# Attention by head pairs: q and k loaded with features along partitions, scores in 64-row halves

## The chip, the cores and the metric

The kernel runs on one core of a Trainium2 chip. Its time is the device time of one launch in microseconds (us); the number given for a kernel is the median of its runs, here three. A profile is one execution recorded by the hardware. Its engines are PE (TensorE matmul; PEld is its weight loads), DVE (VectorE), ACT (ScalarE), POOL (GpSimd) and SP (SyncE, which issues the DMAs).

## The reference

Causal attention over B, H, S, D = 4, 8, 576, 64 is mixed with a read from a memory matrix; two feed-forward layers follow. All inputs are fp32 except the last layer's weights, which come as 64-bit words.

```python
scores = where(causal, -1e9, q @ k.T / sqrt(D)); a = softmax(scores); local = a @ v
q_p = phi(q)                                  # phi(x) = where(x > 0, x, exp(x) - 1) + 1
mem_out = (q_p @ M_prev) / (q_p . z_prev + 1e-6)
attn = g * mem_out + (1 - g) * local          # g = sigmoid(beta), one per head
x = attn as (2304, 512)                       # tokens x features
P = exp(x @ w_gate - max); 8 rounds of scaling P by its row sums and column sums
out = sum_e P[:, e] * (relu(x @ w1[e]) @ w2[e])
return leaky_relu(out @ w_in) @ w_out
```

## The kernel before, in words

Every fp32 operand of a matmul is split into a rounded part "h" and the rest "l"; a product takes three matmuls, h·h, h·l and l·h. ACT makes the rounded part by a copy to fp32r, and DVE or POOL subtracts to get the rest.

Class Attention works on 16 pairs of heads (4 batches of 4 pairs), one head (j = 0, 1) at a time. `load` fetches q, k, v token by token, in runs of 64 numbers. `transposed` turns q, k and the features phi(q) on PE and splits them. `scores` computes five blocks of rows t = 0..4 of a head: t = 0 to 3 are 128 rows each against all keys up to them, t = 4 is the tail: the last 128 rows (448 to 575), whose first half repeats rows of t = 3. In batch 0 a score block takes three matmuls; later batches stack the two parts of k on the two halves of the partitions (`stacked`), and two matmuls do. `softmax` adds the mask and takes the row maximum in one DVE instruction per block and then the exponential on ACT. `normalize` scales the blocks by the reciprocal sums, `turn` transposes the weights of the head before in three groups ("r", "x", "y") on PE, with ACT and DVE making the two parts, `outputs` multiplies them with v and adds the memory read, and `collect` puts the result into xh, xl and DRAM.

`body` runs it in stages. In the first, attention of batch 0 has the core alone, with weight pieces of expert 0 being split beside it (`W.advance`). From ("done", 0) on, `fill` puts steps of class First (expert 0's first layer, m1_products at L514, and second layer, m2_products at L522, 256 tokens at a time) between the attention steps, as many as `FILL` says per step and as far as the finished batches reach (`ready`). After attention come the gate and the Sinkhorn rounds, again with what is left of First as filler, and then `rest`, which has experts 1 to 7 and the last layer.

PSUM in the first stage: three "big" tiles of two banks and two "one" tiles of one bank. In the second: two big, one "one", two for po and one for ph (L1073, L1074, L1090). Outside `rest` the Tile framework orders each engine's instructions itself by its own estimates and priorities, so the order of the code isn't the order on an engine.

Of the kernel before, what the change touches and what calls it, by code (L numbers as in the profile page):

```python
# [27 lines left out]
def f32(ap):  # L28
    return ap.bitcast(F32)
# [31 lines left out]
class Attention:  # L61
# [4 lines left out]
    def __init__(self, tc, ctx, xh, xl, xd, q, k, v, M_prev, z_prev, ident, g_bc, iomg_bc):  # L66
        self.tc, self.nc = tc, tc.nc
        self.xh, self.xl, self.xd = xh, xl, xd
        self.q, self.k, self.v, self.M, self.z = q, k, v, M_prev, z_prev
        self.ident, self.g, self.iomg = ident, g_bc, iomg_bc  # L70
# [7 lines left out]
        self.at = {}  # L78
        for nm, pad, n in (("r", 128, 384), ("x", 64, 512), ("y", 128, 768)):
            hi = self.sb.tile([P, pad + n], F32R, name=f"at_{nm}h")  # L80
            lo = self.sb.tile([P, pad + n], F32R, name=f"at_{nm}l")
            for t in (hi, lo):
                nc.vector.memset(f32(t[:, :pad]), 0.0)
            self.at[nm] = (hi, lo, pad, n)


        self.nv = self.sb.tile([P, 5, 2, D], F32, name="nv")
        nc.gpsimd.memset(self.nv[:D, 4], 0.0)


        self.ks = [self.sb.tile([P, S], F32R, name=f"k{j}") for j in range(2)]
        self.qz = [[self.sb.tile([P, S], F32R, name=f"q{part}{j}") for part in "hl"] for j in range(2)]
        self.ms = [self.sb.tile([P, P], F32R, name=f"ms{j}") for j in range(2)]
        for j in range(2):
            for t in (*self.qz[j], self.ms[j]):
                nc.gpsimd.memset(f32(t[D - j * D:P - j * D]), 0.0)
# [4 lines left out]
    ones = "rx"  # L101

    def one(self, nm):
        return self.ps1.tile([P, 512], F32, tag="one", name=nm)

# [3 lines left out]
    def load(self, b, hp):  # L109
        nc, h0 = self.nc, 2 * hp  # L110
        r = {"b": b, "hp": hp}
        for nm, src in (("q", self.q), ("k", self.k), ("v", self.v)):
            t = self.nv if nm == "v" else self.sbt([P, 5, 2, D], "n" + nm)
            for j in range(2):
                nc.sync.dma_start(out=t[:, 0:4, j, :], in_=src[b, h0 + j, 0:512, :].rearrange("(c p) d -> p c d", p=P))
            o = D if nm == "v" else 0
            nc.sync.dma_start(out=t[o:, 4], in_=src[b, h0:h0 + 2, S - P + o:S, :].rearrange("h p d -> p h d"))
            r[nm] = t
            if nm == "q":
                z = self.sbt([P, 2, D], "nz")  # L120
                nc.sync.dma_start(out=z, in_=self.z[b:b + 1, h0:h0 + 2].to_broadcast([P, 2, D]))
        m = self.sbt([P, D], "nm")
        nc.sync.dma_start(out=m, in_=self.M[b, h0:h0 + 2].rearrange("h p d -> (h p) d"))
        r["z"], r["m"] = z, m
        return r

    def transposed(self, r, nm):

        nc = self.nc
        ps = self.big("tps")  # L130
        for c in range(5):
            q0 = 448 if c == 4 else c * P
            nc.tensor.transpose(ps[:, P + q0:2 * P + q0], r[nm[0]][:, c].rearrange("p h d -> p (h d)"), self.ident)
        rows = (slice(0, D), slice(D, P))
        stacked = self.stacked(r)
        if nm == "qT":
            for j, ((hi, lo), s) in enumerate(zip(self.qz, rows)):
                nc.scalar.activation(hi[s], ps[s, P:P + S], AF.Copy)
                if stacked:
                    nc.sync.dma_start(out=f32(hi[rows[1 - j]]), in_=f32(hi[s]))  # L140
            for (hi, lo), s in zip(self.qz, rows):
                nc.vector.tensor_sub(lo[s], ps[s, P:P + S], f32(hi[s]))
        elif nm == "kT" and stacked:
            for t, s in zip(self.ks, rows):
                nc.scalar.activation(t[s], ps[s, P:P + S], AF.Copy)
            for j, (t, s) in enumerate(zip(self.ks, rows)):
                nc.vector.tensor_sub(t[rows[1 - j]], ps[s, P:P + S], f32(t[s]))
        else:
            hi, lo = self.ks if nm == "kT" else [self.sbt([P, S], "pT" + part, F32R) for part in "hl"]
            nc.scalar.activation(hi, ps[:, P:P + S], AF.Copy)  # L150
            nc.vector.tensor_sub(lo, ps[:, P:P + S], f32(hi))
            r[nm] = hi, lo

    @staticmethod
    def stacked(r):
        return r["b"] > 0

    def features(self, r):

        nc = self.nc  # L160
        ph, z, h0 = r["q"], r["z"], 2 * r["hp"]
        r["p"] = ph
# [14 lines left out]
        nc.gpsimd.tensor_mul(ph3, ph3, nrm.rearrange("p c h -> p (c h)").unsqueeze(2).to_broadcast([P, 10, D]))  # L177

    def values(self, r):

        nc = self.nc
        vs = self.sbt([P, 2, 5, P], "vs", F32R)
        for j in range(2):
            o = D if j else 0
            nc.vector.tensor_copy(vs[:, j, :, o:o + D], r["v"][:, :, j, :])
            nc.gpsimd.tensor_sub(vs[:, j, :, D - o:P - o], r["v"][:, :, j, :], f32(vs[:, j, :, o:o + D]))
        for j, ms in enumerate(self.ms):
            o, s = (D if j else 0), slice(j * D, (j + 1) * D)
            nc.vector.tensor_copy(ms[s, o:o + D], r["m"][s])
            nc.vector.tensor_sub(ms[s, D - o:P - o], r["m"][s], f32(ms[s, o:o + D]))  # L190
        r["vs"] = vs

    def head(self, r, j):
        sm, nm = self.sbt([P, 5], "sm", bufs=2), self.sbt([P, 5], "nm_", bufs=2)
        return {"r": r, "j": j, "a": {}, "sm": sm, "nm": nm}

    def scores(self, s, t, ps, o):

        nc, r, j = self.nc, s["r"], s["j"]
        q0 = 448 if t == 4 else t * P  # L200
        n = S if t == 4 else (t + 1) * P
        (qh, ql), (ka, kb) = self.qz[j], self.ks
# [5 lines left out]
    def softmax(self, s, t, ps, o):  # L208
        nc = self.nc
        n = S if t == 4 else (t + 1) * P  # L210
        a = self.sbt([P, n], f"a{t}", bufs=2)
        mo = 64 if t == 4 else 512 - P * t
        nm, sm = s["nm"][:, t:t + 1], s["sm"][:, t:t + 1]
        nc.vector.tensor_tensor_reduce(out=a, in0=ps[:, o:o + n], in1=self.mask[:, mo:mo + n], scale=-0.125, scalar=3.0e38,  # L214
                                       op0=ALU.add, op1=ALU.min, accum_out=nm)
        nc.scalar.activation(a, a, AF.Exp, bias=nm, scale=-1.0, accum_out=sm)  # L216
        s["a"][t] = a

    def normalize(self, s, t0, t1):
        nc, h = self.nc, 2 * s["r"]["hp"] + s["j"]  # L220
        sl = s["sm"][:, t0:t1]
        nc.vector.tensor_scalar(out=sl, in0=sl, scalar1=1e-9, scalar2=self.iomg[:, h:h + 1], op0=ALU.add, op1=ALU.mult)
        nc.vector.reciprocal(sl, sl)
        for t in range(t0, t1):
            a = s["a"][t]
            if t < 3:
                nc.vector.tensor_scalar(out=a, in0=a, scalar1=s["sm"][:, t:t + 1], scalar2=None, op0=ALU.mult)
            else:
                nc.scalar.activation(a, a, AF.Copy, scale=s["sm"][:, t:t + 1])  # L229

    BLOCKS = {"r": ((1, 1), (0, 0), (1, 0)),
              "x": ((3, 3), (4, 3), (2, 0), (3, 0), (4, 0)),
              "y": ((4, 4), (2, 1), (3, 1), (4, 1), (2, 2), (3, 2), (4, 2))}

    def turn(self, s, nm):

        nc = self.nc
        hi, lo, pad, n = self.at[nm]
        ps = self.one("atps") if nm in self.ones else self.big("atps")
        o = b = 64 if nm == "y" else 0  # L240
# [937 lines left out]
```

## Time and profile before

| | us |
|---|---|
| median of 3 runs | 2236.69 (2234.03 to 2238.33) |
| profiled execution, from its first to its last instruction | 2234.6 |
| PE busy / DVE busy / ACT busy / POOL busy | 2165.0 / 1562.9 / 870.0 / 1108.8 |
| first matmul of First; first matmul of the gate; first matmul of `rest` | 113.4; 417.5; 522.2 |

No time of the profiled execution outside its span is given; the span lies 2.1 us under the median and inside the range of the runs, and it is what the sums are made against. A matmul's record holds a pipeline time beside its columns and overlaps the next record, so PE's work is read from the distance of starts and not from the busy time. Durations on other engines overlap a little too.

### The profile page before, as it was taken

The page shows a single profiled execution, that of the slowest core. Times are in us where ns is not written, and L with a number is a line of the kernel's source. Part 1 is how long each engine was busy: PE and PEld are TensorE (multiplying, and loading weights), DVE is VectorE, ACT ScalarE, POOL GpSimd, SP SyncE. Part 2 cuts the span into 40 slices and gives each one's busy share as a digit, 9 for nine tenths or more (in the row PEclk, how much of TensorE's full clock was granted, in tenths as well). Part 3 has the DMA queues.
Part 4 walks back from the last instruction along what each step waited for, and adds up shares of the span by engine and source line. Part 5 has one row for each costly group of instructions (what it writes and reads, how often), then busy time and mean ns, then how long its engine had stood idle before and what let it go on. Part 6 is the DMA issues. An engine that isn't in the chain of part 4 may idle for free.

```text
span 2234.6 us, 36326 instructions
## 1 busy us (share of the span) xinstructions
PE 2165.0 (97%) x13973; PEld 1938.1 (87%) x13973; DVE 1562.9 (70%) x2904; ACT 870.0 (39%) x1753; POOL 1108.8 (50%) x993
## 2 busy tenths in 40 slices
PE   6799999989999999999999999999999999999999
PEld 5688889778888999998998988889898988898898
DVE  8989899565877777777777788855555554566565
ACT  7877777433332222223222233332333233332421
POOL 5132222244775455455444568854555543665550
PEclk9999999999999999999999999999999999999999
DMA  5233332224542222222124634421111152336111
GB/s 138 63 89 94 92 96 82 68 90 147 161 142 67 67 67 76 76 67 67 57 71 152 213 116 135 125 72 52 57 51 45 57 201 68 109 95 227 66 57 38
DMA packets 215757, 213.01 MB, mean 95 GB/s; under 512 B 71968, under 2 KB 169248, under 8 KB 214048
## 3 DMA queue, kind: packets, MB, share of 16 engines
q1 hardware_dynamic: 215584, 210.69, 30.4%
q8 instruction: 110, 1.80, 0.3%
q14 instruction: 63, 0.52, 0.1%
HBM read 157.83 MB, written 49.28 MB: 93 GB/s over the span
## 4 chain that ended last, share of the span: by engine, by line
PE 76%; DVE 9%; issue 5%; ACT 4%; POOL 4%; DMA 2%; SPq 0%; POOLq 0%; DVEq 0%; ACTq 0%
PE po L882 35%; PE pq L839 27%; PE pq L827 4%; PE ph L514 3%; PE po L522 2%; PE sps L206 2%; PE atps L245 1%; ACT a L229 1%; PE avps L261 1%; POOL stl L687 1%; DVE a L214 1%; ACT a L216 1%; DMA xa<-xd 1%; DVE x L277 1%; ACT x L270 0%
## 5 line engine op out<-in xcount | busy, mean ns | idle before, releaser
L882 PE MATMUL po<-w,hh 128*128 128x512 f32 x2592 | 810.6, 393 | 7.9 <-ACT acc L894 3.1
L882 PEld LDWEIGHTS po<-w,hh 128*128 128x128 f32 x2592 | 473.9, 188 | 106.2 <-DVE acc L892 3.3
L882 PE MATMUL po<-w,hl 128*128 128x512 f32 x1296 | 509.4, 393 | 0.0
L629 POOL TENSOR_TENSOR w0l<-raw,w0h 128x512 fp32r<-128x512 f32 x144 | 191.3, 1349 | 360.3 <-ACT w0h L628 360.3
L857 ACT ACTIVATE hh<-c 128x512 fp32r<-128x512 f32 x224 | 129.2, 624 | 476.0 <-DVE c L852 476.0
L882 PEld LDWEIGHTS po<-w,hl 128*128 128x128 f32 x1296 | 243.6, 188 | 56.1
L839 PE MATMUL pq<-Xh,w0h 128*128 128x256 f32 x960 | 266.2, 277 | 2.1 <-DVE uv L847 1.4
L839 PE MATMUL pq<-Xl,w0h 128*128 128x256 f32 x960 | 265.3, 276 | 0.0
L839 PE MATMUL pq<-Xh,w0l 128*128 128x256 f32 x960 | 265.1, 276 | 0.0
L858 DVE SCALAR_TENSOR_TENSOR hl<-c,hh 128x512 fp32r<-128x512 f32 x224 | 169.3, 797 | 79.3 <-ACT hh L857 79.3
L892 DVE SCALAR_TENSOR_TENSOR acc<-po,Pm,acc 128x512 f32<-128x512 f32 x252 | 178.4, 748 | 49.3 <-PE po L882 47.4
L629 POOL TENSOR_TENSOR w<-raw,w 128x512 fp32r<-128x512 f32 x144 | 199.8, 1405 | 1.7 <-ACT w L628 1.7
L847 DVE TENSOR_TENSOR uv<-pq,s 128x256 f32<-128x256 f32 x144 | 60.5, 420 | 191.8 <-ACT s L846 191.6
L839 PEld LDWEIGHTS pq<-Xh,w0h 128*128 128x128 f32 x960 | 180.1, 188 | 7.3 <-DVE uv L847 2.0
L839 PEld LDWEIGHTS pq<-Xl,w0h 128*128 128x128 f32 x960 | 180.2, 188 | 4.1
L839 PEld LDWEIGHTS pq<-Xh,w0l 128*128 128x128 f32 x960 | 180.2, 188 | 0.0
L846 ACT ACTIVATE s<-pq 128x256 f32<-128x256 f32 x144 | 54.9, 381 | 256.1 <-PE pq L839 256.0
L629 POOL TENSOR_TENSOR ql<-raw,qh 128x512 fp32r<-128x512 f32 x48 | 62.8, 1329 | 129.8 <-ACT qh L628 129.8
L861 ACT ACTIVATE hh<-c 128x512 fp32r<-128x512 f32 x64 | 40.5, 632 | 185.9 <-DVE c L860 185.9
L839 PE MATMUL pq<-Xh,w1h 128*128 128x256 f32 x384 | 106.1, 276 | 1.1 <-ACT xa L957 1.1
L839 PE MATMUL pq<-Xh,sh 128*128 128x256 f32 x384 | 106.0, 276 | 0.0
L839 PE MATMUL pq<-Xl,sh 128*128 128x256 f32 x384 | 106.0, 276 | 0.0
(325 smaller groups left out, 5557.4 us busy)
## 6 DMA issues: line engine op xcount, KB each, us to landing
raw<-in_moe_w_dram SPq DMA_DIRECT2D x136, 512.0 KB, 3.6
Xh<-kh SPq DMA_DIRECT2D x6, 1792.0 KB, 7.4
Xl<-kl SPq DMA_DIRECT2D x6, 1792.0 KB, 11.5
f<-in_moe_w_in_dram SPq DMA_DIRECT2D x16, 512.0 KB, 5.0
f<-in_moe_w_out_dram SPq DMA_DIRECT2D x16, 512.0 KB, 4.7
raw<-wide_in SPq DMA_DIRECT2D x16, 512.0 KB, 3.4
raw<-wide_out SPq DMA_DIRECT2D x16, 512.0 KB, 3.7
kh<-sth SPq DMA_DIRECT2D x12, 512.0 KB, 5.2
```

What stands on the lines that cost most here:

```text
L206: nc.tensor.matmul(ps[:, o_:o_ + kn], x[:, q0:q0 + P], y[:, k0:k0 + kn], start=(i == 0), stop=(i == len(terms) - 1))
L514: nc.tensor.matmul(ph[:, :T], wp[:, c, f0:f0 + P], x[:, c, t0:t0 + T], start=(n == 0), stop=(n == 11))
L522: nc.tensor.matmul(po, a[:, s], wp[:, c, :], start=(first and n == 0), stop=(last and n == 2))
L629: self.nc.gpsimd.tensor_sub(lo, src, f32(hi))
L827: nc.tensor.matmul(ph[:, f * SB:(f + 1) * SB], wp(a, c % 2), xp[x][:, c], start=(n == 0), stop=(n == 11))
L839: nc.tensor.matmul(b[-1][:, o:o + SB], wp(a, c), X[s][part][:, x, c], start=(n == 0), stop=(n == 5))
L846: nc.scalar.activation(s1, b[0][:, lo], AF.Copy)
L847: v.tensor_add(uv[:, 0], b[0][:, up], s1)
L857: nc.scalar.activation(hh[:, f], c, AF.Relu)
L858: v.scalar_tensor_tensor(out=hl[:, f], in0=c, scalar=0.0, in1=f32(hh[:, f]), op0=ALU.max, op1=ALU.subtract)
L882: nc.tensor.matmul(po[j], a[:, f, r], w[1, part][:, f], start=(fp == 0 and f == 0 and n == 0), stop=(fp == 1 and f == 1 and n == 2))
L892: nc.vector.scalar_tensor_tensor(out=acc[t], in0=po[j], scalar=Pm[:, t0 + t, e:e + 1], in1=acc[t], op0=ALU.mult, op1=ALU.add)
```

## The change

q and k come already laid out with the 64 features of the two heads of a pair along the 128 partitions (`lay_out`, on the host, moves numbers and computes none), so PE no longer turns them; `split` makes their parts, ACT the rounded one and POOL the rest. A pair's two heads go through the steps together. For t = 0 to 3 `scores` issues, for each of the three products, one matmul on partitions 0 to 63 for the first head and one on 64 to 127 for the second, into different banks. The tail (t = 4) holds the last 64 rows of both heads in one tile of 128 rows, with q as a block-diagonal operand (`bd`), which POOL copies together. `turn` has four groups, ordered as the score stages, each for both heads at once. The features are computed from a second, token-by-token copy of q (`qn`). The weight splits of M (L184, L185 after the change) go from DVE to POOL. q and k parts, `at` and the score tiles have one buffer each. PSUM: four big tiles in the first stage; in the second two big, two for po and two for ph, and the "one" tiles are gone.

```diff
+    def split(self, r):
+        nc = self.nc
+        for n in "qk":
+            (hi, lo), raw = self.qk[n], r["raw" + n]
+            nc.scalar.activation(hi, raw, AF.Copy)
+            nc.gpsimd.tensor_sub(lo, raw, f32(hi))
+        for t, x in zip(self.bd, self.qk["q"]):
+            for j in range(2):
+                s = slice(j * D, (j + 1) * D)
+                nc.gpsimd.tensor_copy(t[s, s], f32(x[s, 512:]))
...
-        terms = ((qh, self.ks[j]), (ql, self.ks[j])) if self.stacked(r) else ((qh, ka), (qh, kb), (ql, ka))
-        for (o_, k0, kn) in (((192, 0, 320), (512, 320, 256)) if t == 4 else ((o, 0, max(n, 256)),)):
-            for i, (x, y) in enumerate(terms):
-                nc.tensor.matmul(ps[:, o_:o_ + kn], x[:, q0:q0 + P], y[:, k0:k0 + kn], start=(i == 0), stop=(i == len(terms) - 1))
+        if ts == (4,):
+            qh, ql = self.bd
+            for o, k0, kn in ((192, 0, 320), (512, 320, 256)):
+                for i, (x, y) in enumerate(((qh, kh), (qh, kl), (ql, kh))):
+                    nc.tensor.matmul(ps[:, o:o + kn], x, y[:, k0:k0 + kn], start=(i == 0), stop=(i == 2))
+            return
+        for n, t in enumerate(ts):
+            w = max((t + 1) * P, 256)
+            for i, (x, y) in enumerate(((qh, kh), (qh, kl), (ql, kh))):
+                for j in range(2):
+                    s, o = slice(j * D, (j + 1) * D), 512 * j + 256 * n
+                    nc.tensor.matmul(ps[:, o:o + w], x[s, t * P:(t + 1) * P], y[s, :w], start=(i == 0), stop=(i == 2))
...
-        group(512, 256, 320, ((0, "x", 256, 320), (3, "x", 0, 256), (1, "y", 256, 320), (2, "y", 576, 320), (4, "y", 0, 256)))
+        group(512, 256, 320, ((0, 64, 320), (1, 384, 320), (2, 704, 320), (3, 1088, 256), (4, 0, 64)))
...
+    STAGES = ((0, 1), (2,), (3,), (4,))
...
+            for k, ts in enumerate(self.STAGES):
+                lo = self.turn(prev, ts) if prev is not None else None
+                yield 1
+                self.scores(r, ts)
+                self.softmax(r, ts)
+                if lo:
+                    lo()
+                if k:
+                    next(f, None)
+                yield 2 if k < 3 else 4
+            if nxt is not None:
+                self.split(nxt)
+                if n + 2 < len(pairs):
+                    self.load_qk(pairs[n + 2])
+            if prev is not None:
+                self.outputs(prev, 0)
+            self.normalize(r)
+            if prev is not None:
+                self.collect(prev, 0)
+            yield 5
...
-FILL = {1: 1, 2: 2, 3: 2, 4: 1, 5: 1, 6: 1, 7: 2}
+FILL = {1: 1, 2: 2, 4: 2, 5: 2, 7: 2}
...
-                with tc.tile_pool(name="pa0", bufs=3, space=PSUM) as att.ps, tc.tile_pool(name="pb0", bufs=2, space=PSUM) as att.ps1:
+                with tc.tile_pool(name="pa0", bufs=4, space=PSUM) as att.ps:
...
-                fph = fx.enter_context(tc.tile_pool(name="e_ph", bufs=1, space=PSUM))
+                fph = fx.enter_context(tc.tile_pool(name="e_ph", bufs=2, space=PSUM))
...
-                with tc.tile_pool(name="pa1", bufs=2, space=PSUM) as att.ps, tc.tile_pool(name="pb1", bufs=1, space=PSUM) as att.ps1:
+                with tc.tile_pool(name="pa1", bufs=2, space=PSUM) as att.ps:
```

On PE, one head of the second stage stood like this (sps are scores, atps the turned weights of the head before, ph and po the first and second layer of First):

```order
L514 MATMUL ph<-xh,w0l_207 128x256
L245 MATMUL atps<-ident,a_1503 128x128
...
L206 MATMUL sps<-k_120,qh_123 128x256
L206 MATMUL sps<-k_120,ql_124 128x256
...
L522 MATMUL po_1404<-w_1_204,hh 128x512 x2
L522 MATMUL po_1404<-w_1_204,hl 128x512
L206 MATMUL sps<-k_120,qh_123 128x384
L206 MATMUL sps<-k_120,ql_124 128x384
L206 MATMUL sps<-k_120,qh_123 128x512
L206 MATMUL sps<-k_120,ql_124 128x512
```

The head's scores are full-height matmuls here, with a group of transposes before or between them. The first two groups of a pair in the same stage stand like this now (lines are those of the changed kernel; L499 and L507 are First's two layers):

```order
L507 MATMUL po_1246<-w_1_179,hl 128x512
L247 MATMUL atps<-ident,a_1228 128x128
...
L499 MATMUL ph<-xh,w0l_182 128x256
L203 MATMUL sps<-kh,qh 128x256 x2
L203 MATMUL sps<-kl,qh 128x256 x2
L203 MATMUL sps<-kh,ql 128x256 x2
...
L247 MATMUL atps<-ident,a_1268 128x128 x3
L247 MATMUL atps<-ident,a_1271 128x128 x3
...
L203 MATMUL sps<-kh,qh 128x384 x2
L203 MATMUL sps<-kl,qh 128x384 x2
L203 MATMUL sps<-kh,ql 128x384 x2
```

A row with x2 is the two halves of the partitions; each group of scores is now a run of such halves with full-height matmuls or transposes around it.

POOL had these rows for a pair in the second stage (nq are the features, vs the parts of v, xl a result's second part):

```order
L177 TENSOR_TENSOR nq<-nq,nrm 128x640
L186 TENSOR_TENSOR vs<-nv,vs 128x5x64 x2
L282 TENSOR_TENSOR xl<-x,xh 128x576
```

and has these now, with the weight splits of expert 0 (L466) among them:

```order
L161 TENSOR_TENSOR nq<-nq,nrm 128x640
L137 TENSOR_TENSOR ql<-rawq,qh 128x576
L466 TENSOR_TENSOR w_0_175<-raw_753,w_0_175 128x512
L141 CAST bdh<-qh 64x64 x2
L141 CAST bdl<-ql 64x64 x2
L137 TENSOR_TENSOR kl<-rawk,kh 128x576
L184 CAST ms_134<-nm 64x64
L185 TENSOR_TENSOR ms_134<-nm,ms_134 64x64
L184 CAST ms_135<-nm 64x64
L185 TENSOR_TENSOR ms_135<-nm,ms_135 64x64
L181 TENSOR_TENSOR vs<-nv,vs 128x10x64
L290 TENSOR_TENSOR xl<-x,xh 128x576
```

The parts ql, bd and kl of the next pair are made here in the order shown, kl last.

## Rows read from the trace of the kernel before

**Rows 1.** Busy time by stage: window, PE, PEld, DVE, ACT, POOL, clock, DMA, GB/s.
```profile
0.00:113.40 113.40, 78.82 (x497) 68.44 (x498) 99.38 (x263) 85.98 (x185) 41.06 (x47) 0.95 0.38 99
22.00:112.00 90.00, 70.56 (x465) 61.92 (x465) 83.46 (x225) 74.17 (x163) 25.27 (x22) 0.96 0.32 84
113.40:417.50 304.10, 294.95 (x2044) 264.75 (x2042) 270.51 (x697) 235.51 (x518) 83.93 (x70) 1.00 0.33 89
417.50:522.20 104.70, 93.86 (x563) 80.67 (x563) 55.96 (x134) 32.66 (x68) 49.75 (x49) 0.97 0.27 86
522.20:2234.60 1712.40, 1697.38 (x10872) 1524.28 (x10872) 1137.04 (x1813) 515.84 (x982) 934.04 (x828) 1.00 0.30 97
```

**Rows 2.** PE in order of time, second stage: start, length, instruction, count.
```profile
201.17 0.28 PE L261 MATMUL avps<-at_yh,vs 128*128 128x256 f32 x1
201.29 0.28 PE L261 MATMUL avps<-at_yl,vs 128*128 128x256 f32 x1
...
203.36 0.63 PE L522 MATMUL po<-w,hh 128*128 128x512 f32 x2
203.82 0.39 PE L522 MATMUL po<-w,hl 128*128 128x512 f32 x1
...
219.24 0.71 PE L245 MATMUL atps<-ident,a 128*128 128x128 f32 x5
219.71 0.36 PE L514 MATMUL ph<-xl,w0h 128*128 128x256 f32 x1
219.91 0.28 PE L514 MATMUL ph<-xh,w0l 128*128 128x256 f32 x1
```

**Rows 3.** PE in order of time around the gate's transposes of 16 rows.
```profile
420.15 0.40 PE L372 MATMUL gps<-xh,wg 128*128 128x512 f32 x1
420.47 0.42 PE L377 MATMUL lg<-ident,lt 16*128 16x16 f32 x4
420.82 0.50 PE L372 MATMUL gps<-xl,wg 128*128 128x512 f32 x1
421.16 0.39 PE L372 MATMUL gps<-xh,wg 128*128 128x512 f32 x1
```

**Rows 4.** DVE by line and shape, 0 to 440: busy, mean ns, idle before.
```profile
L248 DVE TENSOR_TENSOR at_yl<-atps,at_yh 128x768 fp32r<-128x768 f32 x32 | 30.5, 953 | 1.7 <-ACT at_yh L247 1.4
L142 DVE TENSOR_TENSOR ql<-tps,qh 64x576 fp32r<-64x576 f32 x32 | 24.1, 753 | 0.6 <-ACT qh L138 0.3
L214 DVE CUSTOM_DVE_ANT_0 a<-sps,mask 128x576 f32<-128x576 f32 x32 | 24.1, 753 | 5.1 <-PE sps L206 5.0
L147 DVE TENSOR_TENSOR k<-tps,k 64x576 fp32r<-64x576 f32 x24 | 18.1, 755 | 1.0 <-ACT k L145 0.3
L190 DVE TENSOR_TENSOR ms<-nm,ms 64x64 fp32r<-64x64 f32 x32 | 10.8, 339 | 0.8
L189 DVE CAST ms<-nm 64x64 fp32r<-64x64 f32 x32 | 8.3, 260 | 1.5 <-PE avps L258 0.7
```

**Rows 5.** ACT by line and shape, 0 to 440.
```profile
L247 ACT ACTIVATE at_yh<-atps 128x768 fp32r<-128x768 f32 x32 | 25.7, 804 | 0.9 <-PE atps L245 0.7
L229 ACT ACTIVATE a<-a,sm 128x576 f32<-128x576 f32 x32 | 24.4, 763 | 0.1
L138 ACT ACTIVATE qh<-tps 64x576 fp32r<-64x576 f32 x32 | 20.6, 645 | 1.3 <-PE tps L133 0.6
```

**Rows 6.** The cast that ends a pair: first and last start; the fourth, by time.
```profile
L280 DVE CAST xh<-x x16: 450/457/1030, 50.2 to 417.5; 128x576 fp32r<-128x576 f32 x16
...
112.84 1.03 DVE L280 CAST xh<-x 128x576 fp32r<-128x576 f32 x1
```

**Rows 7.** PE in order of time: the first turn of the kernel.
```profile
26.30 1.80 PE L245 MATMUL atps<-ident,a 128*128 128x128 f32 x15
```

**Rows 8.** POOL by line and shape, 0 to 440.
```profile
L481 POOL TENSOR_TENSOR w0l<-raw,w0h 128x512 fp32r<-128x512 f32 x18 | 26.3, 1470 | 59.2 <-ACT w0h L480 50.4 <-PE ph L514 8.8
L282 POOL TENSOR_TENSOR xl<-x,xh 128x576 fp32r<-128x576 f32 x16 | 22.9, 1432 | 20.8 <-DVE xh L280 20.8
```

More of the change, by code (lines that the diff above doesn't have):

```diff
@@ L77, in __init__ @@
         self.mask = mask
[L78 to L88, printed above, removed]
@@ L91, in __init__ @@
[L91 to L96 removed]
+        tail = self.sb.tile([P, S], F32, name="tail")
+        nc.gpsimd.memset(tail, 0.0)
@@ new lines, in __init__ @@
+        nc.sync.dma_start(out=tail[:D, 512:], in_=mask[:D, 512:512 + D])
+        nc.sync.dma_start(out=tail[D:, 512:], in_=mask[:D, 512:512 + D])
+        self.tail = tail
+        self.inv = self.sb.tile([P, HP, 9], F32, name="inv")
+        for hp in range(HP):
+            for j in range(2):
+                c = iomg_bc[:, 2 * hp + j:2 * hp + j + 1]
+                nc.gpsimd.tensor_copy(self.inv[:, hp, j:8:2], c.to_broadcast([P, 4]))
+                r = slice(j * D, (j + 1) * D)
+                nc.gpsimd.tensor_copy(self.inv[r, hp, 8:9], c[r])
@@ L98, in big @@
+        for t in self.at:
+            nc.vector.memset(f32(t[:, :, 1024:1152]), 0.0)
+            nc.vector.memset(f32(t[:, :, 1344:1472]), 0.0)
     def big(self, nm):
         return self.ps.tile([P, 1024], F32, tag="big", name=nm)
-    ones = "rx"
-    def one(self, nm):
-        return self.ps1.tile([P, 512], F32, tag="one", name=nm)
     def sbt(self, shape, nm, dt=F32, bufs=1):
         return self.sb.tile(shape, dt, tag=nm, name=nm, bufs=bufs)
[L109 to L113, printed above, removed]
-            for j in range(2):
[L115 to L152, printed above, removed]
@@ L177, in features, with turned @@
         nc.gpsimd.tensor_mul(ph3, ph3, nrm.rearrange("p c h -> p (c h)").unsqueeze(2).to_broadcast([P, 10, D]))
+        yield
+    def turned(self, r):
+        nc = self.nc
+        ps = self.big("tps")
+        for c in range(5):
+            q0 = 448 if c == 4 else c * P
+            nc.tensor.transpose(ps[:, P + q0:2 * P + q0], r["p"][:, c].rearrange("p h d -> p (h d)"), self.ident)
+        hi, lo = r["pT"] = [self.sbt([P, S], "pT" + part, F32R) for part in "hl"]
+        nc.scalar.activation(hi, ps[:, P:P + S], AF.Copy)
+        nc.vector.tensor_sub(lo, ps[:, P:P + S], f32(hi))
@@ L219, in normalize @@
[L219 to L225, printed above, removed]
+        vs = r["vs"] = self.sbt([P, 10, P], "vs", F32R)
+        v = r["v"].rearrange("p j c d -> p (j c) d")
+        nc.vector.tensor_copy(vs[:, :, :D], v)
+        nc.gpsimd.tensor_sub(vs[:, :, D:], v, f32(vs[:, :, :D]))
@@ new lines, in softmax @@
+    def softmax(self, r, ts):
+        nc, ps = self.nc, r["sps"]
+        if ts == (4,):
+            jobs = [(4, 0, 192, S, self.tail, 8)]
+        else:
+            jobs = [(t, j, 512 * j + 256 * n, (t + 1) * P, self.mask[:, 512 - P * t:640], 2 * t + j) for n, t in enumerate(ts) for j in range(2)]
+        for t, j, o, n, mask, i in jobs:
+            a = r["a"][t, j] = self.sbt([P, n], f"a{t}{j}")
+            nm = r["nm"][:, i:i + 1]
+            nc.vector.tensor_tensor_reduce(out=a, in0=ps[:, o:o + n], in1=mask, scale=-0.125, scalar=3.0e38,
+                                           op0=ALU.add, op1=ALU.min, accum_out=nm)
+            nc.scalar.activation(a, a, AF.Exp, bias=nm, scale=-1.0, accum_out=r["sm"][:, i:i + 1])
@@ L228, in normalize @@
             else:
[L229 to L235, printed above, removed]
-        nc = self.nc
-        hi, lo, pad, n = self.at[nm]
-        ps = self.one("atps") if nm in self.ones else self.big("atps")
-        o = b = 64 if nm == "y" else 0
-        for (t, c) in self.BLOCKS[nm]:
-            k0 = 448 if c == 4 else c * P
-            if t == 4 and c < 4:
-                o -= D
-            nc.tensor.transpose(ps[:, o:o + P], s["a"][t][:, k0:k0 + P], self.ident)
-            o += P
-        nc.scalar.activation(hi[:, pad:], ps[:, b:b + n], AF.Copy)
-        return lambda: nc.vector.tensor_sub(lo[:, pad:], ps[:, b:b + n], f32(hi[:, pad:]))
@@ L253, in outputs @@
+    def outputs(self, r, j):
+        nc = self.nc
+        av = r["av"] = self.big("avps")
         rows = slice(j * D, (j + 1) * D)
@@ L281, in collect @@
             nc.sync.dma_start(out=self.xd[:, hp, c0:c0 + S], in_=r["x"])
-            self.late = lambda: nc.gpsimd.tensor_sub(self.xl[:, hp, c0:c0 + S], r["x"], f32(self.xh[:, hp, c0:c0 + S]))
-    late = None
+            nc.gpsimd.tensor_sub(self.xl[:, hp, c0:c0 + S], r["x"], f32(self.xh[:, hp, c0:c0 + S]))
+    STAGES = ((0, 1), (2,), (3,), (4,))
     def run(self):
-        pairs = [(b, hp) for b in range(B) for hp in range(HP)]
-        r = self.load(*pairs[0])
-        self.transposed(r, "qT")
-        self.transposed(r, "kT")
-        for _ in self.features(r):
-            pass
-        prev = f = None
-        for n in range(len(pairs)):
-            last = n + 1 == len(pairs)
-            for j in range(2):
-                s = self.head(r, j)
-                lo = self.turn(prev, "r") if prev is not None else None
-                ps = self.big("sps")
-                self.scores(s, 0, ps, 0)
-                self.scores(s, 1, ps, 512)
-                self.softmax(s, 0, ps, 0)
-                self.softmax(s, 1, ps, 512)
+        pairs = [{"b": b, "hp": hp, "a": {}} for b in range(B) for hp in range(HP)]
+        self.load_qk(pairs[0])
+        self.load_n(pairs[0])
+        self.load_v(pairs[0])
+        self.split(pairs[0])
+        self.load_qk(pairs[1])
+        prev = None
+        for n, r in enumerate(pairs):
+            nxt = pairs[n + 1] if n + 1 < len(pairs) else None
+            r["sm"], r["nm"] = self.sbt([P, 9], "sm", bufs=2), self.sbt([P, 9], "nm_", bufs=2)
+            f = self.features(r)
+            for k, ts in enumerate(self.STAGES):
[3 more added lines that the diff above has]
+                self.softmax(r, ts)
@@ L305, in run @@
                 if lo:
                     lo()
-                yield 1
-                if f is not None:
-                    for _ in f:
-                        pass
-                    f = None
-                lo = self.turn(prev, "x") if prev is not None else None
-                ps = self.big("sps")
-                self.scores(s, 2, ps, 0)
-                self.scores(s, 3, ps, 512)
-                self.softmax(s, 2, ps, 0)
-                self.softmax(s, 3, ps, 512)
-                if lo:
-                    lo()
@@ L320, in run @@
-                yield 2
-                lo = self.turn(prev, "y") if prev is not None else None
-                ps = self.big("sps")
-                self.scores(s, 4, ps, 192)
-                self.softmax(s, 4, ps, 192)
-                if lo:
-                    lo()
-                yield 3
-                if j == 1 and not last:
-                    self.transposed(nxt, "qT")
-                if prev is not None:
-                    self.outputs(prev)
-                self.normalize(s, 0, 5)
@@ L352, in run @@
-                prev = s
-            r = nxt
-        for nm in "rxy":
-            self.turn(prev, nm)()
+                if k:
[10 more added lines that the diff above has]
+                self.collect(prev, 0)
@@ L356, in run @@
+            yield 5
+            if prev is not None:
+                self.outputs(prev, 1)
+                self.collect(prev, 1)
+                if prev["hp"] == HP - 1:
+                    yield ("done", prev["b"])
+            self.values(r)
+            self.turned(r)
+            if nxt is not None:
+                self.load_n(nxt)
+                self.load_v(nxt)
+            yield 4
+            prev = r
+        for ts in self.STAGES:
+            self.turn(prev, ts)()
             yield 7
-        self.outputs(prev)
@@ L358, in run @@
-        self.collect(prev)
-        self.late()
+        for j in range(2):
+            self.outputs(prev, j)
+            self.collect(prev, j)
         yield ("done", B - 1)
```

162 lines of the change are left out of this document (90 added, 72 removed).

## The prediction

> **What bounds the kernel now.** I read the busy time by stage first. [rows 1] cut the span at the first matmul of First (113.4), of the gate (417.5) and of `rest` (522.2). `rest` takes 1712.4 us, PE is busy for 99% of it, and the change leaves its code alone. So the change acts on the first 522.2 us, 417.5 of which hold attention.
>
> In the first stage (the row from 22 to 112) DVE is busy for 83.46 of 90 us, 93%, ACT for 74.17, 82%, PE for 78%, POOL for 28%: DVE bounds it, with ACT close behind. In the second stage PE is busy for 294.95 of 304.1 us, but its records overlap, so I then read PE in order of time. In [rows 2] a matmul of 256 columns starts 0.12 us after the one before, two of 512 take 0.46 (0.23 each), five transposes 0.47 (0.094 each), and the matmul behind transposes takes 0.20 where its likes take 0.12: 0.08 for each change from transposes. Between 256 and 512 columns I interpolate: 320 take 0.148, 384 take 0.175.
>
> With these distances I add up what PE is asked to do in the second stage, from the counts of the program's order. First: 540 x 0.12 + 270 x 0.23 = 126.9. Scores, 23 heads of six at 256, two at 320, two at 384, two at 512: 23 x 1.83 = 42.0. Transposes: 522 x 0.094 = 49.1. Outputs, 24 heads of ten at 256 and eight at 320: 57.2. Changes: 95 groups of transposes x 0.08 = 7.6. Together 282.8, so PE waits for 21.3 of 304.1 us, 7%. PE bounds the second stage by its work, and DVE (270.51, 89%) is near.
>
> **First stage, part by part.** A pair ends with the cast to xh; the first is at 50.2 and the fourth at 112.84, so a pair takes 62.6 / 3 = 20.9 us [rows 6]. At 93% that is 19.4 us of DVE for a pair, and at 82% 17.2 of ACT.
>
> DVE loses, for each pair of batch 0: the rest of q, two at 0.753; the rest of k, one at the same length (L147's 0.755); the parts of M, 2 x (0.260 + 0.339) = 1.2; one of two tail blocks, 0.753; and about 0.2 in the turned weights, whose six instructions of 3328 columns become four of 3200 at 953 ns for 768 [rows 4]. That is 4.4, and leaves 15.0. ACT loses two copies of q at 0.645 and one of k, gains two copies of the same width at about 0.65, and loses one tail's scaling (0.763), one tail's exponential of the same size and some 0.2 in the turned weights (804 ns for 768 columns) [rows 5]: 2.4, leaving 14.8.
>
> POOL gains two subtractions of 128x576 at 1.432 [rows 8] and eight small ones (64x64), which cost DVE 0.26 to 0.34 each [rows 4]; I count 0.3, with 0 and 0.5 as ends. 5.9 us per pair (25.27 of 90) become about 11: not the bound.
>
> Two engines at 15 us that wait for each other will not reach today's 93%. The bounds are 15.0 / 0.927 = 16.2 and 20.9 (nothing gained). The mean of today's two shares, 0.875, gives 17.1; I take 17.5.
>
> First's matmuls start when pair 4 is through. The first turn comes at 26.30 now [rows 7]; in the changed kernel it waits for both heads of pair 0 instead of one, but for fewer preparations ahead of them, so I take 24, with 20 and 30 as ends. 24 + 4 x 17.5 = 94 instead of 113.4.
>
> **Second stage.** Counted the same way from the changed order:
> First, 572 x 0.12 + 276 x 0.23 = 132.1 (the new `FILL` gives a pair 16 steps instead of 15). Transposes 355 x 0.094 = 33.4, with 59 changes x 0.08 = 4.7. Outputs 56.0: the tail's matmul on 256 columns becomes one of 64, taken at the 0.094 of a 128-column transpose. Tails, 11 pairs of three at 320 and three at 256: 8.8.
>
> The scores in halves are 264 matmuls, 24 to a pair: 12 at 256, six at 384, six at 512. The trace shows no two matmuls on different halves of the partitions, so this is bounded. One after another they take 11 x 3.87 = 42.6. If two halves always run together, half of that, 21.3. In between stands the weight load that each needs: transposes, each with a load, follow each other at 0.094 [rows 2], so two loads take 0.19, and a pair of halves takes 0.19 at 256 and 384 columns and 0.23 at 512: 11 x 2.4 = 26.4. I take this one, as it rests on a row.
>
> Each group of halves also changes the height of the array in use. The only rows of that are the gate's transposes of 16 rows [rows 3]: they start 0.32 after a 512-column matmul (0.23 by itself), and the next takes 0.34: 0.09 in, 0.11 out. 35 groups x 0.20 = 7.0.
>
> [...]
>
> The sum is 132.1 + 33.4 + 4.7 + 56.0 + 8.8 + 26.4 + 7.0 = 268.4. With the same 7% of waiting: 288.6.
>
> What could make new waits here? q's and k's parts have one buffer, and the second part of k is the last that POOL makes at a hand-over. Behind the tail's scores PE has 1.4 of First, 4.7 of outputs, 1.4 of First, 0.5 of transposes, 1.4 of First, 0.6 of turning and 0.7 of First before the next pair's scores: 10.6 us. POOL needs, after ACT's copy (0.65), the rest of q, four small copies and the rest of k, with at worst two weight splits (1.470) ahead [rows 8]: 0.65 + 2.9 + 1.2 + 1.4 + 1.4 = 7.6. Hidden; a POOL that is 3 us later would show, with PE standing at that matmul and First's filler queued behind it. On DVE the load falls by 5 us a pair, so what is late next is PE's own work.
>
> **Third stage and rest.** 2.7 steps of First's first layer and one of its second have moved ahead: (572 - 540) x 0.12 + (276 - 270) x 0.23 = 5.2 less of 104.7, so 99.5. The loads now move q, k, v in whole rows and the copy of q's parts between partitions is gone; loads are issued a pair ahead, and I count neither as gain. `rest` stays at 1712.4.
>
> **The sum.** 94 + 288.6 + 99.5 + 1712.4 = 2194.5, against the profiled 2234.6: 40.1 less, about 19 of it in the first stage, 15 in the second, 5 in the third, which is work moved forward. The median of the runs shown, 2236.7, is 2.1 above the profiled execution; 2236.7 - 40 = 2197.
>
> **Rivals.**
> Halves in turn: nothing runs together, the 42.6 stay. 284.6 / 0.93 = 306.0, 17 more: 2214. For it: no row shows an overlap. Against it: the two halves use other rows of the array and other banks.
>
> Halves fully together: 263.3 / 0.93 = 283.1, 5.5 less: 2191. [...]
>
> Buffers: with the "one" tiles gone, turned weights and scores share two big tiles in the second stage, and each turn must pass ACT and DVE before the next begins. If PE's waiting doubles to 14%, 268.4 / 0.86 = 312, 23 more: 2220. For it: a pair still passes 11 big tiles through two buffers, and each now holds two heads. Against it: before it was 13, and DVE now has slack.
>
> Slower: each change from one half to the other drains. Successive matmuls alternate halves; if each waited out the pipeline time of the one before, 0.28 - 0.12 = 0.16 [rows 2], 264 x 0.16 = 42.2 come on top of halves in turn: 326.8 / 0.93 = 351, 63 more: 2259. It cancels the gain from 0.08 per half on. For it: [rows 3] have a cost of 0.1 at a change of height. [...]
>
> No gain in the first stage (ACT bound, with DVE waiting for it): 24 + 4 x 20.9 = 107.6, 14 more: 2210; with halves in turn or buffers it reaches 2228 to 2234.
>
> **How the numbers follow.** Forecast 0.56, its own range 2183 to 2208; halves in turn 0.16; buffers 0.15; halves together, with shorter waits than 7%, 0.07; draining 0.06. The low end is halves together, 4% of waiting (263.3 / 0.96 = 274) and pairs of 16.2: 2177, and with 20 instead of 24 for the first turn 2173. The high end is halves in turn or buffers, with most of the first stage's gain missing: 2228. A measurement of this kernel can tell about 0.2%, 4.5 us, from no change. Slower holds the draining and a rest, 0.07; within 0.2% are two failures at once, 0.04; faster 0.89.
>
> **What would show it.** First's first matmul near 94; a pair every 17.5 us before it and every 24 or so after; the gate near 383. In PE's order of time a pair of halves of 512 columns should take 0.23 and one of 256 about 0.19: 0.46 and 0.24 mean halves in turn. ACT and DVE should both be near 85% in the first stage. I am wrong if PE waits much more than 7% of the second stage, if its scores stand on POOL's rest of k, or if `rest` moves.

## The result, and the profile after

The changed kernel takes 2207.82 us, median of four runs (2206.66 to 2209.78), against 2237.07 in the runs beside it: a ratio of 0.9871, 95% interval 0.9857 to 0.9885. The forecast was 2197; 29 us came instead of 40, and the time lies 0.2 us inside the upper end of the stated range (2183 to 2208). The profiled execution has a span of 2204.9 us.

The busy time by stage, cut where [rows 1] are cut (First's first matmul, the gate, `rest`); columns as there, the first row again without the start:

```profile
22.00:107.70 85.70, 61.72 (x384) 50.66 (x385) 81.21 (x170) 64.28 (x139) 52.85 (x70) 0.82 0.38 112
107.70:387.00 279.30, 275.66 (x1967) 241.28 (x1967) 211.55 (x517) 196.81 (x428) 129.03 (x162) 0.99 0.32 94
387.00:491.00 104.00, 91.11 (x527) 78.20 (x525) 56.51 (x131) 31.83 (x66) 50.25 (x49) 0.93 0.28 86
491.00:2204.90 1713.90, 1697.31 (x10872) 1524.40 (x10872) 1136.43 (x1814) 515.70 (x982) 933.46 (x828) 1.00 0.30 97
```

| stage | before | forecast | after | miss |
|---|---|---|---|---|
| to First | 113.4 | 94 | 107.7 | +13.7 |
| to the gate | 304.1 | 288.6 | 279.3 | -9.3 |
| to `rest` | 104.7 | 99.5 | 104.0 | +4.5 |
| `rest` | 1712.4 | 1712.4 | 1713.9 | +1.5 |

So the gain lies in the second stage (24.8 of 29.7 in the spans), and the first, where most was forecast, gave 5.7. In the first stage DVE is as full as before (95%, 93% before), the granted clock of TensorE fell from 0.96 to 0.82, and POOL went from 28% to 62%.

PE in order of time in the second stage, as [rows 2]: one pair's scores in halves of 256, 384 and 512 columns, the last with First's matmuls around them.

```profile
206.89 0.50 PE L203 MATMUL sps<-kl,qh 64*128 64x256 f32 x2
207.12 0.39 PE L203 MATMUL sps<-kh,ql 64*128 64x256 f32 x2
207.24 0.40 PE L203 MATMUL sps<-kh,qh 64*128 64x256 f32 x2
207.35 0.40 PE L203 MATMUL sps<-kl,qh 64*128 64x256 f32 x2
...
211.04 0.33 PE L203 MATMUL sps<-kl,qh 64*128 64x384 f32 x2
211.21 0.34 PE L203 MATMUL sps<-kh,ql 64*128 64x384 f32 x2
...
214.79 0.28 PE L499 MATMUL ph<-xh,w0l 128*128 128x256 f32 x1
214.99 0.50 PE L203 MATMUL sps<-kh,qh 64*128 64x512 f32 x2
215.33 0.40 PE L203 MATMUL sps<-kl,qh 64*128 64x512 f32 x2
215.56 0.39 PE L203 MATMUL sps<-kh,ql 64*128 64x512 f32 x2
215.89 0.73 PE L507 MATMUL po<-w,hh 128*128 128x512 f32 x2
216.46 0.39 PE L507 MATMUL po<-w,hl 128*128 128x512 f32 x1
```

Each row of scores is two halves, and from the second row of a group on rows start 0.117, 0.17 and 0.23 apart: a pair of halves takes what one matmul of that width takes alone. The weight loads don't show: 0.117 stands at 256 columns where the prediction had estimated 0.19 for two of them.

The change of height shows in four places. First's matmul of 256 columns takes 0.20 to the first halves (0.12 by itself: 0.08 more), the first halves of 512 take 0.34 (0.11 more), the last ones 0.33 (0.10 more), and the two full-height matmuls behind them 0.57 (0.46 by themselves: 0.11 more). That is 0.40 for a group, twice the 0.20 that was read from the gate's transposes. The second stage has 35 such runs of halves, two of them a single matmul; in the other 33 the four come to 0.38 to 0.40, 0.39 in the median.

The first stage: the cast that ends a pair ([rows 6]), then PE's two long waits at its start (in brackets the idle time and what ended it; the first is the first turn, [rows 7]), then some of DVE's and POOL's rows at one pair's end, by time.

```profile
48.80 1.47 DVE L288 CAST xh<-x 128x576 fp32r<-128x576 f32 x1
70.09 0.45 DVE L288 CAST xh<-x 128x576 fp32r<-128x576 f32 x1
88.90 0.46 DVE L288 CAST xh<-x 128x576 fp32r<-128x576 f32 x1
106.70 1.11 DVE L288 CAST xh<-x 128x576 fp32r<-128x576 f32 x1
```

```profile
23.05 1.54 PE L247 MATMUL atps<-ident,a 128*128 128x128 f32 x6 [5.67 <-DVE a L225]
28.28 0.58 PE L203 MATMUL sps<-kl,qh 64*128 64x256 f32 x2 [3.19 <-POOL kl L137]
```

```profile
60.33 1.42 POOL L137 TENSOR_TENSOR ql<-rawq,qh 128x576 fp32r<-128x576 f32 x1 [0.81 <-POOL ms L185]
60.74 1.03 DVE L157 TENSOR_SCALAR nrm<-nrm 128x10 f32<-128x10 f32 x1
61.68 0.56 POOL L141 CAST bdh<-qh 64x64 fp32r<-64x64 f32 x2
62.19 4.92 DVE L225 TENSOR_SCALAR a<-a,sm 128x128 f32<-128x128 f32 x6
62.32 1.42 POOL L137 TENSOR_TENSOR kl<-rawk,kh 128x576 fp32r<-128x576 f32 x1
63.68 0.53 POOL L141 CAST bdl<-ql 64x64 fp32r<-64x64 f32 x2
64.29 1.27 POOL L466 TENSOR_TENSOR w1l<-raw,w1h 128x512 fp32r<-128x512 f32 x1
65.52 1.37 POOL L161 TENSOR_TENSOR nq<-nq,nrm 128x640 f32<-128x640 f32 x1
```

After the first turn at 23.05 (forecast 24) the pairs take 25.7, 21.3, 18.8 and 17.8 us; forecast was 17.5 for each. Two things stand out. In this stretch POOL works through without a gap, and part of what PE waits for stands in that queue: k's rest (3.19, and 4.95 before it for the very first scores) and the product for the features at its end. From 14 us on to First, PE's waits that the profile lists are 9.4 us for POOL (6.2 of it for that product) and 18.6 for DVE. And some of DVE's instructions between SBUF tiles are stretched while POOL runs: one on ten elements takes 1.03 (0.16 at its shortest), and six scalings take 4.92 where six at the median of all 96 (347 ns) take 2.1.

### The profile page after: what moved, and what is told of

It reads as the page before. It is cut to its first block, busy times and chain, and to the rows that moved or that the text cites. A ratio compares the mean times of both kernels' runs of the same rounds, so it can differ in the third digit from the quotient of the medians.

```text
span 2204.9 us, 35500 instructions
## 1 busy us (share of the span) xinstructions
PE 2131.9 (97%) x13781; PEld 1899.0 (86%) x13781; DVE 1498.6 (68%) x2666; ACT 821.8 (37%) x1645; POOL 1183.0 (54%) x1151
## 4 chain that ended last, share of the span: by engine, by line
PE 74%; DVE 5%; issue 3%; POOL 3%; ACT 1%; DMA 1%; POOLq 0%; DVEq 0%; ACTq 0%
PE po L867 37%; PE pq L824 28%; PE pq L812 4%; PE po L507 1%; PE ph L499 1%; PE avps L271 1%; DVE hl L843 1%; POOL w0l L614 0%; DMA xa<-xd 0%; DVE acc L877 0%; DVE c L845 0%; PE atps L247 0%; DVE c L834 0%; POOL ql L614 0%; PE xt L929 0%
## 5 line engine op out<-in xcount | busy, mean ns | idle before, releaser
L824 PE MATMUL pq<-Xl,w1h 128*128 128x256 f32 x384 | 106.0, 276 | 0.0
L824 PE MATMUL pq<-Xh,w1l 128*128 128x256 f32 x384 | 106.0, 276 | 0.0
```

The lines of the kernel that those rows point to most:

```text
L824: nc.tensor.matmul(b[-1][:, o:o + SB], wp(a, c), X[s][part][:, x, c], start=(n == 0), stop=(n == 5))
```

## Experiments

Two theories for the first stage. SHARED: DVE stands still while POOL works, and DVE bounds. LATE: POOL's results come too late, since they stand in one queue.

**The subtractions on DVE.**
```
-            nc.gpsimd.tensor_sub(lo, raw, f32(hi))
+            nc.vector.tensor_sub(lo, raw, f32(hi))
```


> The two subtractions of the split of q and k go from POOL to DVE, nothing else. In the changed kernel DVE's six scalings of a pair (L225) take 3.9 to 5.2 us in the first stage, 0.81 us each, against 0.35 each in the second stage and in the kernel before; they lie beside POOL's split. Theory SHARED (DVE's scaling and casts stand still while POOL works): the scalings fall back to about 2.1 us a pair where no weight split runs, 2 x 0.75 us of subtraction come on top, so a pair of the first stage gets 2 us shorter; First's first matmul at 98 to 102 instead of 107.7, the whole 2198 to 2203. Theory LATE (POOL's results come late for PE, the scalings are long for another reason): the scalings keep 0.8 each, the pair gains only PE's wait for the rest of k; First at 104 to 108, the whole 2204 to 2210.

Measured 2199.35, ratio to before 0.9833 (0.9818 to 0.9848); First starts at 102.3. The time is SHARED's, First 0.3 behind it. But the waits for k's rest are gone too, and the scalings are short only in the two pairs without weight splits (2.7 for six; 6.05 in the pair with them). LATE's numbers failed, its mechanism did not.

**The same, and POOL subtracts for nobody.**
```
+            if 4 * r["b"] + r["hp"] < 5:
+                nc.gpsimd.tensor_sub(self.xl[:, r["hp"], 3 * S:4 * S], raw, f32(hi))
```


> As the kernel with the subtractions on DVE, but for the first five pairs POOL also does the same two subtractions into a place that nobody reads (rows of xl that are written anew later). SHARED: the scalings are stretched again, 3.5 to 5 us for six, First's first matmul 105 to 113, the whole 2206 to 2214. LATE: nobody waits for those results, so as with the subtractions on DVE alone, within 2 us.

Measured 2210.7, ratio 0.9889 (0.9873 to 0.9906); First at 115.4. The number is again SHARED's; the rows leave it open. DVE's scalings to 120 us, by line (busy, mean ns), without the idle subtractions and with them; then PE's longest entry among the waits (sum, times, longest) up to First, again without and with:

```profile
L225 DVE TENSOR_SCALAR a<-a,sm 128x128 f32<-128x128 f32 (+2 forms) x30 | 18.4, 676 | 0.1
```
```profile
L227 DVE TENSOR_SCALAR a<-a,sm 128x128 f32<-128x128 f32 (+2 forms) x30 | 19.4, 710 | 0.2
```
```profile
PE tps L170 <- POOL nq L161: 9.5, 3, 4.4
```
```profile
PE tps L172 <- POOL nq L163: 18.7, 4, 7.8
```

The scalings grew by 1 us, PE's wait for the features' product by 9.2. Nobody reads the idle results, but what PE needs stands behind them; I had overlooked that, so this run doesn't exclude LATE. It doesn't show LATE alone either: that product also needs DVE's instructions on ten elements, and one of them was stretched beside the idle work (again without and with, busy us, mean ns):

```profile
L159 DVE TENSOR_TENSOR nrm<-nrm,g 128x10 f32<-128x10 f32 x6 | 1.1, 180 | 0.0
```
```profile
L161 DVE TENSOR_TENSOR nrm<-nrm,g 128x10 f32<-128x10 f32 x5 | 5.0, 994 | 0.0
```

A late queue and a DVE that stands still would both delay the product, and this run doesn't separate them.

**The scalings in a form that isn't stretched**, with a sum that nobody reads; POOL as it was.
```
-  nc.vector.tensor_scalar(out=a, in0=a, scalar1=sm[:, i:i + 1], scalar2=None, op0=ALU.mult)
+  nc.vector.tensor_scalar(out=a, in0=a, scalar1=sm[:, i:i + 1], scalar2=0.0, op0=ALU.mult, op1=ALU.add,
+                          accum_out=r["nm"][:, i:i + 1])
```


> Nothing moves between engines; DVE's six scalings of a pair also add up their rows into a column that nobody reads, which is another form of the same instruction. [...] Estimate for the six without any standing still, at the softmax's one-pass times on DVE (0.28, 0.41, 0.54 and 0.08 for each read of the sum): 2.9 us, against 3.9 to 5.2 now. [...] LATE: 2207 to 2211.

Beside POOL's subtraction of k the six now take their own time; three of them:

```profile
42.07 1.43 POOL L137 TENSOR_TENSOR kl<-rawk,kh 128x576 fp32r<-128x576 f32 x1
42.15 0.34 DVE L225 TENSOR_SCALAR_CACHE_REDUCE a<-a,sm 128x128 f32<-128x128 f32 x1
...
42.42 0.48 DVE L225 TENSOR_SCALAR_CACHE_REDUCE a<-a,sm 128x256 f32<-128x256 f32 x1
...
43.22 0.61 DVE L225 TENSOR_SCALAR_CACHE_REDUCE a<-a,sm 128x384 f32<-128x384 f32 x1
```

Over all 96 the instructions take 0.33 to 0.61, in both stages; why this form isn't stretched was not shown. DVE's share up to First falls from 93% to 84% (78.33 of 92.8 us from 14 on). Yet First starts at 106.8, 0.9 earlier, where 1.0 to 2.3 us less for the six of each of four pairs (2.9 for 3.9 to 5.2) would be 4 to 9; the runs below that leave this stage alone differ from the changed kernel by up to 0.6. Measured 2203.74, ratio 0.9852 (0.9838 to 0.9867), below LATE's range, but in an interval that overlaps the changed kernel's; 2.6 us of the difference in the profiles lie in `rest`, which the edit leaves alone. So the stretching of the scalings is real, and by itself was not what held the stage.

**Both edits in the first five pairs.**


> For the first five pairs both edits at once: q's and k's subtractions on DVE, and the scalings in the form with a sum. In the first alone scalings still met weight splits on POOL (3.5, about 4 and 6.1 us for six where 2.7 stand without). SHARED: the six at 2.4 to 2.9 in each pair, 1 + 1 + 3 us less in three of them, First's first matmul at 96 to 99, the whole 2193 to 2197. If what is left is ACT or PE's work at the lower clock, First at 100 to 102 and the whole 2197 to 2200.

Measured 2194.83, ratio 0.9822 (0.9802 to 0.9842); First at 99.0, as expected. Alone the edits brought 5.4 and 0.9 of the first stage, together 8.7: DVE's stretching counts once POOL's subtractions are out of the way. It is still 5 us over the forecast's 94: the first turn comes at 18.5, before the forecast's 24, but the pairs take 23.6, 21.1, 18.7 and 16.3 us instead of 17.5 each.

**No fine parts for the first weights** (they stay zero).
```
+                if i < 6:
+                    nc.vector.memset(f32(lo[:, s]), 0.0)
+                else:
+                    nc.gpsimd.tensor_sub(lo[:, s], r[:, s], f32(hi[:, s]))
```


> In the changed kernel POOL splits twelve half pieces of First's weights at 1.3 us each before First starts, most of them in the first two pairs after the first turn; those pairs take 25.8 and 21.3 us, the two behind them, with hardly any weights, 18.8 and 17.8 (forecast: 17.5). This kernel leaves out the fine parts of the first six pieces (DVE writes zeros in their place), so POOL has only the attention's work. If the weights in front of q's and k's rests and of the features' product on POOL make the first two pairs long: the first turn at 20 to 22, the pairs 22 to 23, 18 to 19, 18 and 18, First's first matmul at 98 to 102, the whole 2197 to 2203. If they are long for another reason (PE at the lower clock, ACT): pairs as now within 1 us, First at 105 to 108, the whole 2204 to 2209.

Measured 2202.21, ratio 0.9846 (0.9826 to 0.9867); First at 104.3, between the two, the whole in the first one's range. The first turn came later (24.5; PE stands 6.81 for k's rest before it), the pairs took 22.2, 20.7, 17.6 and 18.2: weights in POOL's queue explain some 3.5 us of the first pair, little of the second. What else makes that one long is open. In the changed kernel the clock is 0.77 and 0.74 in the first two pairs, 0.95 and 0.88 in the others, 1.00 in the first three before. That the clock makes the second pair long is not shown: with the scalings in the other form it was 0.82 there and the pair took 21.4, with both edits 0.78 and 21.1. With both edits the first pair took 23.6 at a clock of 0.83.

**One half after the other.**
```
-            for i, (x, y) in enumerate(((qh, kh), (qh, kl), (ql, kh))):
-                for j in range(2):
+            for j in range(2):
+                for i, (x, y) in enumerate(((qh, kh), (qh, kl), (ql, kh))):
```


> The scores do all three products of one half and then all three of the other, where they alternate between the halves now; the same 24 matmuls to a pair. If halves of one kind cannot lie beside each other and unlike ones do, of six matmuls only the third and the fourth overlap: 5 distances instead of 3, so 11 x 1.93 x 5/3 = 35.5 instead of 21.3 in the second stage, 14 us more, and the whole 2218 to 2224. If the gain does not come from the overlap, the gate stays at 387 within 3 us and the whole at 2205 to 2210.

Measured 2206.74, ratio 0.9866 (0.9852 to 0.9881), the second stage 279.6; First starts at 110.8, 3.1 later, for a reason that stays open. The time is that of the second theory, its reason isn't: the overlap is still there. Program order is three products of head 0, then three of head 1; PE in order of time:

```profile
209.24 0.38 PE L203 MATMUL sps<-kh,qh 64*128 64x256 f32 x1
...
210.62 0.38 PE L203 MATMUL sps<-kl,qh 64*128 64x256 f32 x1
210.63 0.38 PE L203 MATMUL sps<-kh,qh 64*128 64x256 f32 x1
210.85 0.28 PE L203 MATMUL sps<-kh,ql 64*128 64x256 f32 x1
210.85 0.28 PE L203 MATMUL sps<-kl,qh 64*128 64x256 f32 x1
210.96 0.28 PE L203 MATMUL sps<-kh,qh 64*128 64x256 f32 x1
210.97 0.28 PE L203 MATMUL sps<-kh,ql 64*128 64x256 f32 x1
```

Head 0's first product ran alone at 209.24. At 210.63 head 1's first product (kh,qh) starts, before head 0's third (kh,ql) at 210.85.

**Both heads from the same half.**
```
-                    s, o = slice(j * D, (j + 1) * D), 512 * j + 256 * n
+                    s, o = slice(0, D), 512 * j + 256 * n
```


> Both heads of a pair take their scores from the first 64 rows (head 1's scores are those of head 0, which this kernel leaves wrong), so all 24 matmuls stand on one half of the array and none can lie beside another. Theory OVERLAP (two halves run at the same time whatever the order of the program, each as a queue of its own): a half of 256 takes 0.12, of 384 0.17, of 512 0.23 by itself, 11 x 3.87 = 42.6 us of scores in the second stage where 21.3 stood, so the gate 18 to 23 us later against First's first matmul, the whole 2224 to 2234 with the first stage (0.5 us a pair of PE, partly hidden). Theory LOADS (the gain came from fewer, larger matmuls and the halves do not matter): second stage 279 to 284, the whole 2206 to 2212.

Two matmuls to a row:

```profile
203.75 0.39 PE L203 MATMUL sps<-kl,qh 64*128 64x256 f32 x2
203.98 0.40 PE L203 MATMUL sps<-kh,ql 64*128 64x256 f32 x2
204.22 0.40 PE L203 MATMUL sps<-kh,qh 64*128 64x256 f32 x2
```

0.235 for two where 0.117 stood. Measured 2236.56, ratio 1.0008 (0.9998 to 1.0018): without the overlap nothing of the gain is left. The second stage is 15.4 longer (expected 18 to 23), the first 15.9 (expected: little). In this kernel, then, PE's scores are on the path in the first stage too; five pairs of halves in turn account for 5 x 3.87 / 2 = 9.7 of it at the full clock, and the rest is open (the granted clock in its four pairs was 0.91, 0.69, 0.74 and 0.95).

**One accumulator for First.** `bufs=2` of `e_ph` becomes 1.


> First's accumulator in PSUM has one buffer in the second stage, as before the change, where the changed kernel has two. The forecast kept the 7% of waiting that PE had before; the trace shows the second stage 9 us shorter than forecast. Theory ROOM (the second buffer took waits away): with one, PE waits for ACT's and DVE's relu at each of some 48 steps of First, 0.05 to 0.2 us each, second stage 283 to 290, the whole 2210 to 2218. Theory OTHER (overlap of the halves and a lighter DVE did it, the buffer nothing): within 2 us of 2208.

Measured 2208.46, ratio 0.9874 (0.9857 to 0.9891), second stage 278.6: OTHER.

**15 steps of First to a pair**: `FILL` has `5: 1` for `5: 2`.


> FILL[5] is 1 instead of 2, so 15 steps of First lie between two pairs' work, not 16; 11 or 12 half steps go from the second stage to the third, about 5 us of PE. Theory CHAIN (the third stage lasts as long as the serial chain of DVE and PE in it, where PE waits some 13 us for DVE; First's work moved out of it saves nothing): second stage 4 to 6 us shorter, the third longer by less than 2, the whole 2202 to 2205. Theory WORK (the third stage is as long as its work, as forecast): the third gains what the second loses, the whole 2206 to 2209.

Measured 2203.26, ratio 0.9855 (0.984 to 0.987). The second stage is 4.4 shorter, the third 2.5 longer: CHAIN's total, its third stage not quite, and the interval overlaps the changed kernel's.

**The edits combined.** Both edits and 15 steps; 13 steps (`4: 1` too); 15 steps with weight pieces moved to the scores.

> The first five pairs with subtractions on DVE and scalings in the form with a sum, and 15 steps of First to a pair instead of 16. If the two gains add up: First at 99, second stage 273 to 275, third 105 to 108, the whole 2189 to 2193; if the third stage takes back what the second loses, 2193 to 2196.

> The same with 13 steps of First to a pair: some 35 half steps, about 15 us of PE, moved from the second stage to the third. CHAIN: the third stage hides about half of it, as with 15 steps, so 3 to 6 us less than with 16 steps, the whole 2188 to 2192. WORK: what can be hidden is used up, and fewer steps leave PE without filling in the second stage, the whole 2194 to 2200.

> As the version with both edits and 15 steps, and in the first stage the weights' pieces are split one at a time beside the scores (where DVE reads PSUM) instead of two at a time at the end of a pair. SHARED: the cast of v (1.2 us, 0.5 alone) and the products on POOL that PE's turning of the features waits for (5 us in the first stage) come earlier: First at 95 to 98, the whole 2186 to 2191. If ACT is in the way of the softmax's exponentials instead, First at 99 to 102, the whole 2191 to 2195.

Measured 2196.76 (ratio 0.9821, 0.9807 to 0.9836), 2203.94 (0.9856, 0.984 to 0.9872) and 2196.99 (0.9824, 0.981 to 0.9839). The first and third can't be told from both edits alone; First starts at 100.8 with the pieces moved, against 98.9, so that was a miss. With 15 steps the two gains don't add up: the time is above both of the expected ranges. With 13 steps the second stage takes 264.7, 13 less than with 16, and the third 22 more: WORK in kind, 4 us above its range, and why the third stage grows by more than what moved there is open. What it hides is used up after about 2 us. The two edits, with 16 steps or 15, beat both kernels, 40 us under the one before.

## Why the prediction was right, and where not

The four errors in the table, +13.7, -9.3, +4.5 and +1.5, leave 10.4 us, and the time lies just inside the range: that is in part luck, since the first stage alone was missed by 13.7.

- **Overlap of the halves.** I took 26.4 us, bounded by weight loads in turn, with 21.3 (fully together) given 0.07. By the distances in the rows it was 21.3, and without the overlap the second stage is 15.4 longer. In the second stage's 130 pairs the two halves started 3 ns apart in the median and at most 16, their weight loads 3 and at most 18.
- **Change of height: mis-sized.** 0.20 a group was forecast, 0.39 measured: 35 groups x 0.39 = 13.7 instead of 7.0. I had read two of the four places from [rows 3], the 0.09 ahead of the 16-row matmuls and the 0.11 behind the first full-height one after them. Between halves no such cost shows: from the second row of a group on, rows of 256 start 0.117 apart where the draining rival put 0.16 on each half.
- **Waiting in the second stage.** With the two terms as measured the sum is 268.4 - 5.1 + 6.7 = 270.0, and 279.3 - 270.0 = 9.3 is left, 3.3% instead of 7%. This is a remainder; the idle time that the profile lists for PE fell from 7.9 to 3.2. So two errors of 5 to 7 us nearly cancel, and the stage beat its forecast because PE waited less. DVE fell from 89% to 76% there; First's second accumulator was not the reason. Two big tiles didn't double the waits.
- **First stage: the step that failed.** "5.9 us per pair become about 11: not the bound" priced POOL by its own sum (52.85 of 85.7 us, 13 a pair). It left out that POOL's queue is a step in each pair's chain, and that DVE's scalings take longer beside POOL (811 ns in the mean of 27, against 347). Taking the two subtractions out of the queue gave back 5.4 us, the first weight splits 3.4, and the subtractions and the scalings' stretching together 8.7. DVE's 15.0 a pair became 79.16 / 4 = 19.8, of which the 27 scalings between 23 and 107.7 account for 27 x (0.811 - 0.347) = 12.5 us in all; taking away this part alone gave 0.9. How the 13.7 us divide between the late queue and DVE's longer instructions is not shown. The cover of 10.6 us for k's rest held in the second stage; at the first two scores of the kernel no outputs stand ahead of them, and PE stood there.
- **Counting the start as a pair.** [rows 6, 7] have 23.9 us from the first turn to the first cast, 3.0 more than a later pair; 4 x 17.5 ignored it. The last two pairs, 18.8 and 17.8, are near 17.5.
- **Third stage.** Work moved forward was to take 5.2 off; it took 0.7. PE waits there for DVE's chain (10.3 us now, 8.5 before), and the run with 13 steps shows that the slack is small.

The rival "no gain in the first stage" came true in its number alone (107.6 forecast for it, 107.7 measured): its reason, ACT as the bound with DVE waiting for it, isn't what the rows show, with DVE at 95% and ACT at 75%. "Halves fully together" came true beside it. The two offset each other in part, which is why the time lies in the range.

## What to carry over

Work moved to an engine with much idle time is priced by what stands behind it in that engine's queue and by which neighbour it holds up, not by its sum: here PE waited 9.4 us for POOL up to First, and DVE's scalings took 811 ns instead of 347. Look at the start of a loop by itself: cover that exists in the steady state was missing there, and PE stood 4.95 and 3.19 us for k's rest. And two 64-row halves were worth laying out, since together they cost what one does (0.117 us at 256 columns, 0.235 with both on one half); each group of them also costs its change of height, here 0.39 us.

## What the runs showed of the hardware

- Matmuls on the two halves of the rows started 16 ns or less apart in all 130 pairs of the second stage, and two of 256 columns took 0.117 us together, 0.235 with both on the same half. With one half's products after the other's in the program, head 1's first started 0.22 us before head 0's third, which precedes it there.
- Each group of 64-row matmuls among full-height ones cost 0.39 us beside its columns (35 groups in 279.3 us): 0.09 to 0.11 ahead of its first matmul, behind that, ahead of the next full-height matmul, and behind that.
- DVE's scaling between SBUF tiles took up to 1645 ns beside POOL (128x384, 412 in the mean of the second stage) and 274 at least (128x128); the same with a running sum 333 to 614 throughout.
